# Four distances, modulo 256 bytes, between the pieces of an expert's first weights and the tokens that stream past them

## The chip, the cores and the metric

The kernel runs on one core of a Trainium2 chip. The metric is device time in microseconds of one execution. A core has TensorE (matmuls: PE in the profile, its weight loads PEld), VectorE (DVE), ScalarE (ACT), GpSimd (POOL) and SyncE (SP, which issues most DMAs), all working on SBUF, a memory of 128 partitions.

## The reference

Retention (linear attention with a decay) over 8 batches of 576 tokens and 8 heads of 64, and behind it a mixture of experts in which each of the 4608 tokens goes to one of 8 experts:

```python
scores = scale * np.matmul(q, k.transpose(0, 1, 3, 2))
ret = scores * Dmat[None]          # gamma ** (i - j), causal
x = np.matmul(ret, v)              # to (4608, 512)
e_idx = np.argmax(x @ w_gate, axis=1)
for e in range(8):                 # mask: the tokens of expert e
    h = np.maximum(x[mask] @ w1[e], 0.0)      # 512 -> 1024
    out[mask] = gate_w[mask, None] * eom[mask, e, None] * (h @ w2[e])
```

## The kernel before

A first stage does the retention in 36 chunks of 128 tokens, chooses the experts and scatters the tokens to a buffer sorted by expert. The second stage goes over the experts. An expert has 616 slots for tokens, in two parts: part 0 of 360 columns and part 1 of 256. Its first product, `mm1`, goes over 8 blocks `fb` of 128 hidden features; its second, `mm2`, over 5 tiles `t` of tokens (four of 128 and, at t = 2, one of 104) and the 8 blocks `fb`.

To get near full precision every operand is held as a high part and the rest (`h` and `l` in the names), and each product is three matmuls on fp32r data: high by high, high by low, low by high. So a call of `mm1` is 12 matmuls (4 blocks `k` of 128 input features by 3), of 360 columns or of 256; a block `fb` of an expert is 12 of each, one part after the other; and an expert has 192 of them, all experts 1536. In a matmul the stationary operand (`lhsT`) is first loaded into the array by a weight load of 128 columns; then the moving operand (`rhs`) streams past. The weight load for the next matmul runs while the current one streams. In `mm1` the weights `w1` are stationary and the tokens `x` (tiles `xh`, `xl`) move; in `mm2` the hidden values (`hh`, `hl`) are stationary and `w2` moves, 512 columns.

`w1` of an expert comes in four pieces `fp` of 256 hidden features: the blocks fb = 2 fp and 2 fp + 1 read piece fp. `start_w` (L128) issues the DMA of a piece into a staging tile `st` and takes two tiles of 4096 bytes per partition from the pool `wpool`, `w1h{fp}` and `w1l{fp}`; `hi_w` (ACT, L142) and `lo_w` (DVE, L147) fill them. The pool has one buffer for each name, so all 8 experts use the same addresses. It lays out tiles in the order in which they are first asked for: the four pieces of `w1`, then the four of `w2` (`wsched` in the first stage gives that order).

Where in 256 bytes a tile begins is set by three small tiles that nothing reads: `shift0` (64 bytes, in the pool ahead), `shift1` (192 bytes, between the pieces of `w1` and of `w2`) and `shift2` (128 bytes, before `x` of part 0). With them the addresses per partition are, modulo 256: all eight `w1` tiles 128 (`w1h0` at 54400), all `w2` tiles 64 (`w2h0` at 87360), `x` of both parts 64 (141120 and 196672), the hidden tiles of both parts 64. Steps inside these tiles are multiples of 512 bytes. So in every matmul of `mm1` the stationary operand begins 64 bytes beyond the moving one, in every one of `mm2` 0 bytes, counted modulo 256.

In the first stage `xnat` (L529) multiplies the retention's output `xT` (stationary, at 224 modulo 256) by `iw` (moving, at 160 for its first block p = 0, and 576 bytes further with each of four blocks p, so at 160, 224, 32 and 96); these matmuls are fp32, not fp32r, and are two passes each.

Of the kernel before, what the change touches and what calls it, by code (L numbers as in the profile page):

```python
# [10 lines left out]
F32 = mybir.dt.float32  # L11
# [15 lines left out]
P = 128  # L27
# [21 lines left out]
def tile_retention_moe(  # L49
# [21 lines left out]
    wpool = ctx.enter_context(tc.tile_pool(name="wpool", bufs=1))  # L71
# [50 lines left out]

    const.tile([P, 16], F32, name="shift0")
    W1, W2 = {}, {}

    def start_w(which, e, fp):  # L128
        src, shape = (w1, [P, KB, 256]) if which == 1 else (w2, [P, 2, DM])
        st = wst.tile(shape, F32, name="st")  # L130
        SP.dma_start(out=st, in_=src[e, fp].rearrange("p (a b) -> p a b", a=shape[1]))
        if which == 2 and not W2:
            wpool.tile([P, 48], F32, name="shift1")
        hi = wpool.tile(shape, F32R, name=f"w{which}h{fp}")
        lo = wpool.tile(shape, F32R, name=f"w{which}l{fp}")
        (W1 if which == 1 else W2)[e, fp] = (hi, lo)
        return st, hi, lo
# [11 lines left out]
    def load_w(which, e, fp):  # L149
        w = start_w(which, e, fp)  # L150
        hi_w(*w)
        lo_w(*w)
# [399 lines left out]
    def weights(g):  # L552
        for w, at in wsched.items():
            if g == at[0]:
                wparts[w] = start_w(w[0], 0, w[1])
            if g == at[1]:
                hi_w(*wparts[w])
# [161 lines left out]
    for t in range(TA, CT):  # L719
        load_rows(0, t)  # L720
    load_idx(0, 1)
    w = [start_w(1, 1, fp) for fp in range(2)]
    fill_slots(1)
    fill_slots(0)
# [56 lines left out]
    with ExitStack() as octx:  # L781
# [3 lines left out]
        with tc.For_i(0, n, 1) as i:  # L785
            e = nc.values_load(ovt[0:1, 0, bass.ds(i, 1)], engines=[mybir.EngineType.SP], min_val=0, max_val=E - 1)
# [102 lines left out]
```

## Time and profile before

| | us |
|---|---|
| median of 3 runs | 608.34 (608.02 to 609.44) |
| profiled execution | 608.83 |
| span of its profile | 607.0 |
| PE busy | 592.4 |
| weight loads (PEld) busy | 529.0 |
| DVE / ACT / POOL busy | 332.8 / 219.3 / 188.1 |

The span goes from the first to the last instruction of the program; the profiled execution has 1.8 us outside it. [...] What a matmul costs the engine is read from start to start. [...]

### The profile page before, as it was taken

The page shows a single profiled execution, that of the slowest core. Times are in us where ns is not written, and L with a number is a line of the kernel's source. Part 1 is how long each engine was busy: PE and PEld are TensorE (multiplying, and loading weights), DVE is VectorE, ACT ScalarE, POOL GpSimd, SP SyncE. Part 2 cuts the span into 40 slices and gives each one's busy share as a digit, 9 for nine tenths or more (in the row PEclk, how much of TensorE's full clock was granted, in tenths as well). Part 3 has the DMA queues.
Part 4 walks back from the last instruction along what each step waited for, and adds up shares of the span by engine and source line. Part 5 has one row for each costly group of instructions (what it writes and reads, how often), then busy time and mean ns, then how long its engine had stood idle before and what let it go on. Part 6 is the DMA issues. An engine that isn't in the chain of part 4 may idle for free. (4 is left out here: it accounts for less than half of the span.)

```text
span 607.0 us, 13986 instructions
## 1 busy us (share of the span) xinstructions
PE 592.4 (98%) x5688; PEld 529.0 (87%) x5688; DVE 332.8 (55%) x735; ACT 219.3 (36%) x477; POOL 188.1 (31%) x235
## 2 busy tenths in 40 slices
PE   8999999999999999999999999999999999999995
PEld 5889888878898999879978987997899799889974
DVE  4599888898760666624543554445265435625410
ACT  1334433323331545324433443433354344325110
POOL 2245544575457515016013301601250110110011
PEclk9999999999999999999999999999999999999999
DMA  9989989875225676444343534444262334221011
GB/s 307 357 301 318 331 289 342 322 265 201 97 91 185 182 197 198 130 128 136 109 138 116 175 104 136 118 136 139 94 188 94 115 107 143 103 84 52 1 38 42
DMA packets 56925, 100.28 MB, mean 165 GB/s; under 512 B 14967, under 2 KB 35832, under 8 KB 56860
## 3 DMA queue, kind: packets, MB, share of 16 engines
q1 hardware_dynamic: 46988, 76.72, 39.6%
q0 software_dynamic: 9440, 21.60, 9.8%
q8 instruction: 45, 0.74, 0.5%
q10 hardware_dynamic: 432, 1.05, 0.5%
q14 instruction: 20, 0.16, 0.1%
HBM read 77.75 MB, written 31.18 MB: 179 GB/s over the span
## 5 line engine op out<-in xcount | busy, mean ns | idle before, releaser
L262 PE MATMUL h_ps<-xh,w1h 128*128 128x360 f32 (+1 forms) x512 | 155.2, 303 | 0.1
L262 PE MATMUL h_ps<-xh,w1l 128*128 128x360 f32 (+1 forms) x512 | 154.9, 303 | 0.0
L262 PE MATMUL h_ps<-xl,w1h 128*128 128x360 f32 (+1 forms) x512 | 154.8, 302 | 0.0
L289 POOL DMA_INDIRECT out_dram<-y,idx x40 | 39.8, 994 | 313.4 <-ACT y L288 268.0
L270 DVE SCALAR_TENSOR_TENSOR hl<-h_ps,hh 128x360 fp32r<-128x360 f32 (+1 forms) x128 | 61.2, 478 | 128.8 <-ACT hh L269 114.4
L283 PE MATMUL y_ps<-w2h,hh 128*128 128x512 f32 (+1 forms) x320 | 125.0, 390 | 0.0
L283 PE MATMUL y_ps<-w2l,hh 128*128 128x512 f32 (+1 forms) x320 | 124.9, 390 | 0.0
L283 PE MATMUL y_ps<-w2h,hl 128*128 128x512 f32 (+1 forms) x320 | 124.6, 389 | 0.0
L269 ACT ACTIVATE hh<-h_ps 128x360 fp32r<-128x360 f32 (+1 forms) x128 | 55.0, 430 | 117.7 <-PE h_ps L262 113.1
L262 PEld LDWEIGHTS h_ps<-xh,w1h 128*128 128x128 f32 x512 | 96.0, 188 | 0.6 <-DVE xl L245 0.3
L262 PEld LDWEIGHTS h_ps<-xl,w1h 128*128 128x128 f32 x512 | 96.1, 188 | 0.3
L262 PEld LDWEIGHTS h_ps<-xh,w1l 128*128 128x128 f32 x512 | 96.1, 188 | 0.0
L288 ACT ACTIVATE y<-y_ps,idx 128x512 f32<-128x512 f32 (+1 forms) x40 | 27.6, 690 | 138.6 <-issue 90.0
L147 DVE TENSOR_TENSOR w1l<-st,w1h 128x512 fp32r<-128x512 f32 x64 | 44.9, 739 | 48.4 <-ACT w1h L142 47.0
L283 PEld LDWEIGHTS y_ps<-w2h,hl 128*128 128x128 f32 (+1 forms) x320 | 58.8, 184 | 14.1
L283 PEld LDWEIGHTS y_ps<-w2h,hh 128*128 128x128 f32 (+1 forms) x320 | 58.8, 184 | 13.8
L283 PEld LDWEIGHTS y_ps<-w2l,hh 128*128 128x128 f32 (+1 forms) x320 | 58.7, 184 | 13.6
L194 POOL DMA_INDIRECT xs<-xgrp,sli x36 | 38.8, 1077 | 62.2 <-issue 21.3
L194 POOL DMA_INDIRECT xs<-zx,fill x42 | 46.1, 1099 | 7.1 <-issue 6.5
L352 POOL TENSOR_TENSOR vp<-pk,gk_sb 128x512 f32<-128x512 f32 x36 | 37.7, 1049 | 30.8 <-PE st_ps L392 12.2
L376 DVE TENSOR_TENSOR S_sb<-sc,cmat_sb 128x512 f32<-128x512 f32 x64 | 41.1, 684 | 11.2 <-PE sc L365 10.7
L147 DVE TENSOR_TENSOR w2l<-st,w2h 128x512 fp32r<-128x512 f32 x64 | 44.7, 737 | 2.3
(128 smaller groups left out, 675.1 us busy)
## 6 DMA issues: line engine op xcount, KB each, us to landing
st<-in_w_dram SPq DMA_DIRECT2D x64, 512.0 KB
pk<-in_pack_dram SPq DMA_DIRECT2D x32, 768.0 KB
x_q<-xs SPq DMA_DIRECT2D x140, 64.0 KB
kn<-in_krow_dram SPq DMA_DIRECT2D x14, 256.0 KB
gq_sb<-in_gq_dram SPq DMA_DIRECT2D x5, 256.0 KB
pk<-in_pack_dram SPq DMA_DIRECT2D x4, 256.0 KB
pk<-in_pack_dram SPq DMA_DIRECT2D x2, 512.0 KB
x_g<-xs SPq DMA_DIRECT2D x4, 256.0 KB
```

The source lines that it names most:

```text
L147: V.tensor_tensor(out=lo[:, k], in0=st[:, k], in1=hi[:, k].bitcast(F32), op=ALU.subtract)
L194: i = G.indirect_dma_start(out=xs, out_offset=bass.IndirectOffsetOnAxis(ap=at, axis=0), in_=x, in_offset=None, **({} if bound is None else ...
L262: i = T.matmul(ps, lhsT=a[:, k, :], rhs=b[:, k, 0:n], start=(j == 0), stop=(j == 3 * KB - 1))
L269: A.activation(out=hh, in_=ps, func=AF.Relu)
L270: V.scalar_tensor_tensor(out=hl, in0=ps, scalar=0.0, in1=hh.bitcast(F32), op0=ALU.max, op1=ALU.subtract)
L283: i = T.matmul(ps, lhsT=a[:, n], rhs=b, start=(j == 0), stop=(j == 3 * FB - 1))
L288: A.activation(out=y, in_=ps, func=AF.Copy, scale=idx.bitcast(F32)[0:m, e, t, 1:2])
L289: G.indirect_dma_start(out=out, out_offset=bass.IndirectOffsetOnAxis(ap=idx[0:m, e, t, 0:1], axis=0), in_=y, in_offset=None, bounds_check= ...
L352: G.tensor_tensor(out=vs[g], in0=pk[g][:, 2].rearrange("p (h d) -> p h d", h=H), in1=gk_sb[:, g % CPB].broadcast_to([P, H, D]), op=ALU.mult)
L376: V.tensor_tensor(out=v(S_sb[:, r].rearrange("p a i -> p (a i)")), in0=v(sc[:, r]), in1=cmat_sb[:, 1:3].rearrange("p c a i -> p a (c i)"). ...
```

## The change

`shift1` goes. In its place three tiles of 64 bytes that nothing reads are taken from the same pool, one before each of the pieces 1, 2 and 3 of `w1`. The pieces then begin at 128, 192, 0 and 64 modulo 256, which is 64, 128, 192 and 0 beyond `x`. The three tiles have 192 bytes together, as `shift1` had, so `w2` and all that follows keep their addresses. No instruction is added, removed or moved.

```diff
     def start_w(which, e, fp):
         src, shape = (w1, [P, KB, 256]) if which == 1 else (w2, [P, 2, DM])
         st = wst.tile(shape, F32, name="st")
         SP.dma_start(out=st, in_=src[e, fp].rearrange("p (a b) -> p a b", a=shape[1]))
-        if which == 2 and not W2:
-            wpool.tile([P, 48], F32, name="shift1")
+        if e == 0 and which == 1 and fp > 0:
+            wpool.tile([P, 16], F32, name=f"shift_{fp}")
         hi = wpool.tile(shape, F32R, name=f"w{which}h{fp}")
         lo = wpool.tile(shape, F32R, name=f"w{which}l{fp}")
```

## Rows read from the trace of the kernel before

**Rows 1.** The page: busy time by engine, share, instructions; the clock by slices.

```profile
PE 592.4 (98%) x5688; PEld 529.0 (87%) x5688; DVE 332.8 (55%) x735; ACT 219.3 (36%) x477; POOL 188.1 (31%) x235
...
PEclk9999999999999999999999999999999999999999
```

**Rows 2.** Busy time by stretch: length, PE, PEld, DVE, ACT, POOL, clock, DMA.

```profile
215.00:600.00 385.00, 384.94 (x2207) 346.67 (x2205) 179.61 (x300) 144.33 (x285) 79.71 (x86) 1.00 0.38 117
```

**Rows 3.** Groups by line and shape: count, busy us, mean ns, idle before.

```profile
L262 PEld LDWEIGHTS h_ps<-xl,w1h 128*128 128x128 f32 x512 | 96.1, 188 | 0.3
...
L262 PE MATMUL h_ps<-xh,w1h 128*128 128x360 f32 x256 | 84.0, 328 | 0.1
...
L262 PE MATMUL h_ps<-xh,w1h 128*128 128x256 f32 x256 | 71.1, 278 | 0.0
```

**Rows 4.** Order of time on PE (start, length), expert 0, 256-column matmuls alone.

```profile
199.35 0.28 PE L262 MATMUL h_ps<-xh,w1h 128*128 128x256 f32 x1
199.47 0.28 PE L262 MATMUL h_ps<-xl,w1h 128*128 128x256 f32 x1
...
207.51 0.28 PE L262 MATMUL h_ps<-xh,w1h 128*128 128x256 f32 x1
```

**Rows 5.** The same view: expert 3, fb = 0, part 1.

```profile
330.43 0.28 PE L262 MATMUL h_ps<-xl,w1h 128*128 128x256 f32 x1
330.55 0.28 PE L262 MATMUL h_ps<-xh,w1l 128*128 128x256 f32 x1
...
331.73 0.33 PE L262 MATMUL h_ps<-xh,w1h 128*128 128x360 f32 x1
```

**Rows 6.** The same view: expert 1, a block of part 0.

```profile
227.04 0.33 PE L262 MATMUL h_ps<-xh,w1h 128*128 128x360 f32 x1
227.21 0.33 PE L262 MATMUL h_ps<-xl,w1h 128*128 128x360 f32 x1
...
228.54 0.28 PE L262 MATMUL h_ps<-xh,w1h 128*128 128x256 f32 x1
```

**Rows 7.** The same view: `mm2`, the tile of 104 tokens and the one behind.

```profile
257.63 0.39 PE L283 MATMUL y_ps<-w2h,hh 128*104 128x512 f32 x1
...
263.13 0.40 PE L283 MATMUL y_ps<-w2h,hh 128*128 128x512 f32 x1
263.36 0.40 PE L283 MATMUL y_ps<-w2l,hh 128*128 128x512 f32 x1
263.60 0.39 PE L283 MATMUL y_ps<-w2h,hl 128*128 128x512 f32 x1
...
265.21 0.39 PE L283 MATMUL y_ps<-w2h,hh 128*128 128x512 f32 x1
...
273.82 0.39 PE L283 MATMUL y_ps<-w2h,hl 128*128 128x512 f32 x1
```

**Rows 8.** All of line 529: shortest, middle and longest row in ns.

```profile
L529 PEld LDWEIGHTS xa<-iw,xT x144: 186/190/192, 15.5 to 167.2; 128*128 128x128 f32 x144
L529 PE MATMUL xa<-iw,xT x144: 284/286/390, 15.6 to 167.3; 128*128 128x144 f32 x144
L529 PEld LDWEIGHTS xb<-iw,xT x144: 190/190/190, 16.0 to 167.7; 128*128 128x128 f32 x144
L529 PE MATMUL xb<-iw,xT x144: 286/286/286, 16.1 to 167.8; 128*128 128x144 f32 x144
```

**Rows 9.** Groups by line and shape, as in Rows 3: the writers of the weights.

```profile
L147 DVE TENSOR_TENSOR w1l<-st,w1h 128x512 fp32r<-128x512 f32 x64 | 44.9, 739 | 48.4 <-ACT w1h L142 47.0
L147 DVE TENSOR_TENSOR w2l<-st,w2h 128x512 fp32r<-128x512 f32 x64 | 44.7, 737 | 2.3
...
L142 ACT CAST w1h<-st 128x512 fp32r<-128x512 f32 x64 | 36.4, 620 | 0.0
L142 ACT CAST w2h<-st 128x512 fp32r<-128x512 f32 x64 | 36.3, 619 | 0.0
```

## The prediction

> **What bounds the kernel now.** Read the page's busy times first: PE has work in flight for 98% of the span, and the clock is at its full level (2.4 GHz) in every slice [rows 1]. The table by stretch sharpens this for the stage of the experts: from 215 to 600 us PE is busy in 384.94 of 385.00 us, while DVE, ACT and POOL are busy in 179.61, 144.33 and 79.71 [rows 2]. So in this stage nothing but TensorE sets the time, and every nanosecond that the change puts on a matmul of `mm1`, or takes off it, is a nanosecond of the span. Since no instruction changes, the only question is the pace of these matmuls.
>
> A row's length doesn't give the pace (278 ns for a 256-column matmul and 328 ns for a 360-column one, [rows 3], overlap their neighbours). The order of time does, from start to start:
> - 256 columns, many alike in a row: from 199.35 to 207.51 us there are 72, so 113.3 ns each [rows 4].
> - 360 columns: from 227.04 to 228.54 us there are 9, so 166.7 ns [rows 6].
> - 512 columns in `mm2`, once settled: 38 in 8.61 us, so 226.6 ns [rows 7].
>
> The 256 and the 512 are in proportion to their columns (twice 113.3 is 226.6), though `mm1` has its operands 64 bytes apart and `mm2` 0. In proportion, 360 columns would take 113.3 x 360/256 = 159.3 ns. They take 7.4 ns more.
>
> **Where the place of an operand could show.** While one matmul streams `x`, the weights of the next are read from the same partitions, in every matmul. Two places in the trace show that the two reads together cost something that neither has alone.
> - The same 256-column matmuls, with the same addresses, also run slower: in the first block of expert 3 there are 11 from 330.43 to 331.73 us, 118 ns each [rows 5] against 113.3 [rows 4]. The clock is full and nothing is waited for. The slow pace lasts through this block and is gone in the next; the first block of each of the experts 1 to 7 has it, which makes seven. So the pair of reads has at least two ways to run side by side, 4.7 ns apart.
> - In `mm2`, weight loads of 104 columns, less to read, go with a slower stream: from 257.63 to 263.13 us 24 matmuls, 229.2 ns each against 226.6. Behind them the 128-column loads start at 235 ns (two from 263.13 to 263.60) and settle to 226.6 only from 265.21 on [rows 7].
>
> Here the Trainium skill speaks against any effect of the change: "SBUF — State Buffer", in "Who interferes with whom", gives TensorE two independent read ports, one for the moving operand and one for weight loads, and says that TensorE never waits on anyone. By that rule the sum of the change would be 0 and the time the one of before. The trace doesn't agree in full: the paces of 118 and 229.2 ns [rows 5, 7] are waits of TensorE's reads that it leaves unexplained.
>
> **The change part by part.**
> - *`shift1` goes, three tiles of 64 bytes come.* Nothing reads or writes them: no instruction, 0 us. Since 3 x 64 = 192 bytes are what `shift1` had, `w2` and the hidden tiles stay 0 apart and the 960 matmuls of `mm2` keep their pace: 0 us.
> - *The writers of the weights.* ACT and DVE write the moved tiles. Today they write `w1` at 128 and `w2` at 64 modulo 256, in 620 against 619 ns and 739 against 737 ns [rows 9]: the place doesn't show, 0 us. If it did, DVE's and ACT's idle time in the stage [rows 2] would hide it. The DMA lands in `st`, which isn't moved.
> - *Piece 0* keeps its 64 bytes: 192 matmuls of each length, 0 us.
> - *Pieces 1, 2 and 3* go to 128, 192 and 0: 3 x 192 = 576 matmuls of 256 columns and 576 of 360. No fp32r matmul of `mm1` in this trace has such a distance, so its price is bounded by rows.
>  - 256 columns: the lower bound is 0, since 113.3 is already in proportion to the 512-column matmuls; the upper is what the worst rows of `mm2` have over their settled pace, 235 - 226.6 = 8.4 ns. Nearest is the slow pace of these very matmuls, 4.7 ns: their stream and the weight load of 128 columns beside it are about equally long, so a disturbed load has little room. I take 4.7: 576 x 4.7 ns = 2.7 us.
>  - 360 columns: between -7.4 (the excess over proportion goes) and +8.4 ns. I take 0. The weight load is the same 128 columns and has 166.7 - 113.3 = 53 ns more room here, so a delay of the load is hidden; a delay of the stream is not, which is why the upper bound stays.
>
> Sum: +2.7 us. On the profiled execution that is 608.83 + 2.7 = 611.5; its own time is 0.5 above the median of the runs, so against the median 608.34 + 2.7 = 611.0 us.
>
> **The rivals.**
> - *The place doesn't matter (608.3).* For it: `xnat`, where the stationary operand lies 64, 0, 192 and 128 beyond the moving one for p = 0 to 3, all four distances of the change. Both pairs have the same middle row, 286 ns, and the same weight load, 190 ns; in the pair at 192 and 128 shortest and longest agree too [rows 8]. The equal pace for each column in `mm1` at 64 and `mm2` at 0 says the same. Against it: these are fp32 matmuls of 144 columns, so the stream is short beside its weight load, and a collision in the longer fp32r streams could pass unseen there; and the two paces of 256 columns [rows 4, 5] differ in nothing but how the reads fall. It decides if the reads settle clear of each other from any start, as the 512-column ones do behind 265.21 us.
> - *The other side: 64 is the poor distance for 360 columns (604.0).* The mechanism: in each 360-column matmul the stream runs once into the weight load beside it and waits 7.4 ns, and at the other distances it doesn't. Price: 576 x 7.4 ns = 4.3 us less, 608.3 - 4.3 = 604.0; with two of the three pieces clear, 384 x 7.4 = 2.8 us less, 605.5. It decides where the gain on the 360 columns exceeds what the 256 lose, that is from 2.7 us, 4.7 ns a matmul. Against it: 256 columns at the same 64 have no such excess, and 360 is the one length that isn't a multiple of 64 columns (256 bytes), so the excess may be its own, whatever the distance.
> - *The forecast, but larger.* Both lengths pay: 4.7 ns on the 256 and 8.4 on the 360 gives 576 x 13.1 ns = 7.5 us, 615.9. This is the upper part of the case slower.
> - *The unread tiles get no room.* Then all pieces would stay at 64 and `w2` alone would move by 192. `shift0` and `shift2` are unread too and stand in the addresses of before; under 0.01, left out.
>
> **How the numbers follow.** Slower (the reads collide at some of the new distances) 0.50; the place doesn't matter 0.32; 64 was the poor one 0.18. I lean to slower over same because there is a second pace [rows 5] with nothing but the meeting of the two reads to explain it, and to slower over faster because the 256 columns have nothing to gain. About 0.2%, 1.2 us, is what a measurement of this kernel can tell from no change; the cases' times lie beyond that on either side, so their chances are those of faster, same and slower. The likeliest time is 611.0. The range goes from 605.5 (two of three pieces gain) to 616.0 (both lengths pay), which leaves out some 0.15 at the two ends.
>
> **What the profile afterwards would show.** Each piece can be read by itself: for fb >= 1 a pair of blocks (12 of 360 columns and 12 of 256) takes 12 x (166.7 + 113.3) = 3360 ns now. Blocks 0 and 1 should keep it; blocks 2 and 3, 4 and 5, 6 and 7 show the price of 128, 192 and 0. By the forecast their 256-column starts are about 118 ns apart and the 360-column ones 166.7; by the first rival all stay at 113.3 and 166.7; by the second the 360 go towards 159.3. The pace of `mm2` should stay at 226.6, the clock full, and PE busy without a gap. The prediction is wrong if blocks 0 and 1 or `mm2` change, if PE gets idle time, or if the price sits in the 360 columns while the 256 keep their pace.

## The result and the profile after

The changed kernel takes 610.14 us (median of 22 runs, 609.50 to 613.17) against 608.85 for the kernel before, measured beside it (22 runs, 607.28 to 610.61). The ratio is 1.0026, 95% interval 1.0019 to 1.0033: 1.6 us slower, between 1.2 and 2.0 (the two medians differ by 1.3). The forecast was 2.7 us slower.

The profiled execution took 609.85 us with a span of 608.1. The page's row of busy times, the row of the stage of the experts, and the groups that answer to [rows 3, 9] (all lines are one further down in the changed kernel):

```profile
PE 593.6 (98%) x5688; PEld 530.5 (87%) x5688; DVE 331.3 (54%) x735; ACT 218.9 (36%) x477; POOL 188.8 (31%) x235
```

```profile
215.00:600.00 385.00, 385.00 (x2201) 347.38 (x2200) 178.89 (x299) 143.40 (x284) 79.54 (x86) 1.00 0.38 117
```

```profile
L263 PE MATMUL h_ps<-xh,w1h 128*128 128x360 f32 x256 | 84.0, 328 | 0.1
...
L263 PE MATMUL h_ps<-xh,w1h 128*128 128x256 f32 x256 | 71.9, 281 | 0.0
...
L148 DVE TENSOR_TENSOR w1l<-st,w1h 128x512 fp32r<-128x512 f32 x64 | 44.9, 738 | 48.4 <-ACT w1h L143 47.0
...
L143 ACT CAST w1h<-st 128x512 fp32r<-128x512 f32 x64 | 36.4, 619 | 0.0
```

As in [rows 1, 2] the stage is TensorE's from end to end, with the clock at its full level, 2.4 GHz (the 1.00 behind POOL's time). Counts are the same; the writers of the weights have their old durations (738 and 619 ns). Only the mean row of a 256-column matmul has moved, from 278 to 281 ns.

What each piece pays is read as the prediction proposed, from the start of one block to the start of the next. In expert 4, blocks fb = 1, 2, 4 and 6 (order of time on PE: start in us, length, operation):

```profile
386.06 0.33 PE L263 MATMUL h_ps<-xh,w1h 128*128 128x360 f32 x1
...
388.05 0.28 PE L263 MATMUL h_ps<-xh,w1h 128*128 128x256 f32 x1
...
389.42 0.32 PE L263 MATMUL h_ps<-xh,w1h 128*128 128x360 f32 x1
...
391.38 0.28 PE L263 MATMUL h_ps<-xh,w1h 128*128 128x256 f32 x1
...
392.81 0.32 PE L263 MATMUL h_ps<-xh,w1h 128*128 128x360 f32 x1
...
396.20 0.33 PE L263 MATMUL h_ps<-xh,w1h 128*128 128x360 f32 x1
...
398.18 0.28 PE L263 MATMUL h_ps<-xh,w1h 128*128 128x256 f32 x1
...
399.60 0.33 PE L263 MATMUL h_ps<-xh,w1h 128*128 128x360 f32 x1
...
403.00 0.33 PE L263 MATMUL h_ps<-xh,w1h 128*128 128x360 f32 x1
...
404.98 0.28 PE L263 MATMUL h_ps<-xh,w1h 128*128 128x256 f32 x1
...
406.42 0.33 PE L263 MATMUL h_ps<-xh,w1h 128*128 128x360 f32 x1
```

Each block is 12 matmuls. From 404.98 to 406.42 twelve of 256 columns at distance 0 take 1.44 us, where twelve at 64 take 1.37 (388.05 to 389.42). All blocks of expert 4, taken to the nanosecond from the same starts (ns for 12 of 360 columns, 12 of 256, and the pair):

| blocks fb | distance | before | after |
|---|---|---|---|
| 0 | 64 | 1999 + 1415 = 3414 | 1998 + 1415 = 3413 |
| 1 | 64 | 1989 + 1372 = 3361 | 1990 + 1375 = 3365 |
| 2 and 3 | 128 | 1988 + 1372 = 3360, both | 1964 + 1421 = 3385; 1968 + 1425 = 3393 |
| 4 and 5 | 192 | 1988 + 1372 = 3360, both | 1984 + 1416 = 3400; 1991 + 1414 = 3405 |
| 6 and 7 | 0 | 1988 + 1372 = 3360, both | 1977 + 1435 = 3412; 1979 + 1435 = 3414 |

The other experts from 1 to 7 repeat this to a few ns. So the six moved blocks pay 8546 - 8232 = 314 ns on their 256 columns and get back 11928 - 11863 = 65 ns on their 360, 249 ns net; in seven experts 1.74 us.

Expert 0 shows the two lengths apart from each other, since its blocks of one part follow one another. First 360 columns at distance 0 (fb = 7), then 256 columns at 64, 128, 192 and 0 (fb = 1, 3, 5 and 7):

```profile
177.65 0.32 PE L263 MATMUL h_ps<-xh,w1h 128*128 128x360 f32 x1
...
179.57 0.39 PE L284 MATMUL y_ps<-w2h,hh 128*128 128x512 f32 x1
...
198.29 0.28 PE L263 MATMUL h_ps<-xh,w1h 128*128 128x256 f32 x1
...
199.65 0.28 PE L263 MATMUL h_ps<-xh,w1h 128*128 128x256 f32 x1
...
201.07 0.28 PE L263 MATMUL h_ps<-xh,w1h 128*128 128x256 f32 x1
...
202.49 0.28 PE L263 MATMUL h_ps<-xh,w1h 128*128 128x256 f32 x1
...
203.91 0.28 PE L263 MATMUL h_ps<-xh,w1h 128*128 128x256 f32 x1
...
205.32 0.28 PE L263 MATMUL h_ps<-xh,w1h 128*128 128x256 f32 x1
...
206.76 0.29 PE L263 MATMUL h_ps<-xh,w1h 128*128 128x256 f32 x1
...
208.20 0.40 PE L284 MATMUL y_ps<-w2h,hh 128*128 128x512 f32 x1
```

Twelve of 256 take 1.36, 1.42, 1.41 and 1.44 us (113.7, 118.2, 117.8 and 120.1 ns each, from the starts to the nanosecond); twelve of 360 at distance 0 take 1.92, which is 160.0 ns each against 166.7 at 64 [rows 6]. Over expert 0 the 256 columns cost 392 ns more than before and the undisturbed 360-column blocks (fb = 3, 4, 6, 7) 202 ns less. Together 1.74 + 0.39 - 0.20 = 1.9 us, within the interval of what was measured. About 0.1 us of the 0.20 is the luck of this execution: in three other traces the blocks at distance 0 (fb = 6 and 7), at the same addresses and behind the same instructions, took 1973 to 1978 ns and not 1920 (see the two parts at different distances). The two profiled spans differ by 1.1 us only, because in this execution expert 1 began 0.7 us earlier (219.10 against 219.78 us).

### The profile page after: what moved, and what is told of

The parts are those of the page before. It is cut to its first block, busy times and chain, and to the rows that moved or that the text cites. A ratio compares the mean times of both kernels' runs of the same rounds, so it can differ in the third digit from the quotient of the medians.

```text
span 608.1 us, 13986 instructions
## 1 busy us (share of the span) xinstructions
PE 593.6 (98%) x5688; PEld 530.5 (87%) x5688; DVE 331.3 (54%) x735; ACT 218.9 (36%) x477; POOL 188.8 (31%) x235
```

## The experiments

Two questions were open: whether it is the distance of the two operands that sets the pace, and not the piece or the place of one operand; and whether the reason given for the price, that only the weight load is delayed and a 256-column matmul has no room to hide it, is the right one. In the table of distances below, (a, b) means that the weights lie a bytes beyond `x` of part 0 (360 columns) and b beyond `x` of part 1 (256 columns), modulo 256.

### The distances dealt to other pieces

`shift0` goes and a fourth tile of 64 bytes stands before `w2`: pieces 0 to 3 at 0, 64, 128, 192.

```diff
-    const.tile([P, 16], F32, name="shift0")
...
-        if which == 2 and not W2:
-            wpool.tile([P, 48], F32, name="shift1")
+        pad = {(1, 1): 16, (1, 2): 16, (1, 3): 16, (2, 0): 16}.get((which, fp)) if e == 0 else None
+        if pad:
+            wpool.tile([P, pad], F32, name=f"shift_{which}{fp}")
```

> The same four distances as in the changed kernel, dealt to other pieces: pieces 0 to 3 at 0, 64, 128 and 192. Theory of the distance: the pairs of blocks of the pieces take about 3413, 3360, 3390 and 3402 ns, the dear pair moves from piece 3 to piece 0; time as the changed kernel, 1 to 2 us over before. Rival (the price sits in the piece, by its place in the row of blocks or in SBUF): the order stays as in the changed kernel, 3360, 3388, 3402 and 3413 for pieces 0 to 3.

Measured: 608.50 us in one run, 606.22 before; pairs of blocks in expert 4: 3353 and 3404 (distance 0), 3376 and 3365 (64), 3385 and 3392 (128), 3400 and 3405 (192). The blocks at 128 and 192 have the same times as in the changed kernel, to 1 ns, though they are other pieces. So it is not the piece. But the dear pair didn't simply move to piece 0: where 3413 was forecast its blocks took 3353 and 3404, and the dearest piece is now the one at 192. The rows (blocks fb = 0 and 1 of expert 4, both at 0) show where the first one gained:

```profile
381.61 0.32 PE L262 MATMUL h_ps<-xh,w1h 128*128 128x360 f32 x1
...
383.53 0.28 PE L262 MATMUL h_ps<-xh,w1h 128*128 128x256 f32 x1
...
384.96 0.33 PE L262 MATMUL h_ps<-xh,w1h 128*128 128x360 f32 x1
...
386.94 0.28 PE L262 MATMUL h_ps<-xh,w1h 128*128 128x256 f32 x1
```

The same 360-column matmuls with the same distance take 1.92 us for twelve behind `mm2` and 1.98 behind 256-column ones. At one distance there is more than one steady pace, and here they go with what ran before.

### Everything 64 bytes further

`shift0` has 128 bytes in place of 64, the three tiles of the change stand between the pieces, and a tile of 192 bytes behind `x` of part 1 moves that pool and the hidden values of part 1 as well. Distances as in the changed kernel, every operand of the experts 64 bytes further.

```diff
-    const.tile([P, 16], F32, name="shift0")
+    const.tile([P, 32], F32, name="shift0")
...
+        pad = {(1, 1): 16, (1, 2): 16, (1, 3): 16}.get((which, fp)) if e == 0 else None
...
+            if e == 0 and part == 1:
+                pl.tile([P, 48], F32, name="shift4")
```

> The distances of the changed kernel piece by piece (64, 128, 192, 0), but w1, x, w2 and the hidden values all lie 64 bytes further in 256. Theory of the distance: every pair of blocks as in the changed kernel within 5 ns (3365, 3385 to 3392, 3400 to 3405, 3413), mm2 at 226.6 ns a matmul. Rival (the place in 256 bytes of one operand by itself decides): the pace of a piece follows the address of w1, so piece 1 (now at 0) shows the 3402 of the piece that was at 0, piece 2 (now at 64) the 3413, and piece 3 (now at 128) the 3360.

Measured: 607.25 us in one run, 606.22 before. Pairs in expert 5: 3413, 3365, 3385, 3392, 3400, 3405, 3413, 3413, the changed kernel's numbers within 1 ns, as in the other experts from 1 to 7. Block fb = 6 of expert 4, whose piece is now at 128 modulo 256, the address that all pieces had before:

```profile
400.38 0.33 PE L265 MATMUL h_ps<-xh,w1h 128*128 128x360 f32 x1
...
402.36 0.28 PE L265 MATMUL h_ps<-xh,w1h 128*128 128x256 f32 x1
...
403.79 0.33 PE L265 MATMUL h_ps<-xh,w1h 128*128 128x360 f32 x1
```

It takes 1.98 and 1.43 us all the same. In these experts the address of one operand by itself doesn't matter; the distance does. Expert 0 differs: there 256 columns at 64 took 1413 and 1416 ns (1372 and 1364 in the changed kernel) and 360 at 0 1973 and 1974 (1920). These are second paces that other kernels show too (below), so they don't speak for the address, but this run alone can't rule it out there. Since the stationary operand is read by weight loads alone, the likely cause is the meeting of a weight load with a stream; no row shows the meeting itself.

### Part 0 at 0, part 1 at 64

The best pace that each length has shown alone, combined: `shift0` and `shift1` go, which puts the weights at 64 like `x` of part 0, and `x` of part 1 goes 64 bytes down.

```diff
-    const.tile([P, 16], F32, name="shift0")
...
-        if which == 2 and not W2:
-            wpool.tile([P, 48], F32, name="shift1")
...
+            if e == 0 and part == 1:
+                pl.tile([P, 16], F32, name="shift4")
...
+        if (e, part, fb) == (0, 1, FB - 1):
+            pools["ht1"].tile([P, 48], F32, name="shift5")
```

> All four pieces of w1 lie 0 bytes (modulo 256) beyond x of part 0 and 64 beyond x of part 1; mm2 keeps its 0. Theory of the distance (the pace of a matmul follows from the distance of its own two operands): the 360-column matmuls go at the 160.0 ns that the blocks 6 and 7 of expert 0 show in the changed kernel, the 256-column ones stay at 113.3; a pair of blocks falls from 3360 to 3280 ns, 56 pairs and expert 0 together give about 5 us less than before, 603.7 us. Rival (the neighbours decide: in experts 1 to 7 of the changed kernel the 360-column matmuls at 0 went at 164.9 ns): a pair of 1978 + 1360 = 3338 ns and 1.2 to 1.8 us less, 607 us. Rival (only the piece, not the distance): no change, 608.8 us.

Measured: 604.29 us (10 runs) against 606.22 (13 runs of the kernel before beside it), ratio 0.9963, 95% interval 0.9947 to 0.9979: 2.2 us faster, the best kernel of this study, but less than half of the 5 us that the distance by itself would give. The rows of expert 0 (360 columns, then 256) and of block fb = 3 of expert 4:

```profile
169.15 0.33 PE L263 MATMUL h_ps<-xh,w1h 128*128 128x360 f32 x1
...
171.12 0.33 PE L263 MATMUL h_ps<-xh,w1h 128*128 128x360 f32 x1
...
201.21 0.28 PE L263 MATMUL h_ps<-xh,w1h 128*128 128x256 f32 x1
...
202.57 0.28 PE L263 MATMUL h_ps<-xh,w1h 128*128 128x256 f32 x1
...
390.83 0.32 PE L263 MATMUL h_ps<-xh,w1h 128*128 128x360 f32 x1
...
392.75 0.28 PE L263 MATMUL h_ps<-xh,w1h 128*128 128x256 f32 x1
...
394.16 0.32 PE L263 MATMUL h_ps<-xh,w1h 128*128 128x360 f32 x1
```

In expert 4 the 360 columns run at 1.92 us for twelve and the 256, at the 64 that gave 1.36 in expert 0, at 1.41, the slow pace of [rows 5]. In expert 0 it is the other way round: the 360 at the slower of their two paces (1.97), the 256 at 1.36. The pair in experts 1 to 7 is 3333 ns, neither the 3280 of the first theory nor the 3338 of the second, which had the slower pace on the other length. Both paces of both lengths exist at these distances; alternating, the two lengths don't reach their better one together.

### The two parts at different distances

The changed kernel's four pieces, with `x` of part 1 moved by 128, 64 and 192 bytes (a tile behind it as above, of 32, 16 and 48 elements, and one behind the hidden values that keeps them in place).

> w1 in the four pieces of the changed kernel, x of part 1 moved by 128 bytes, so that the distances of the 360- and the 256-column matmuls are (64,192), (128,0), (192,64) and (0,128) for pieces 0 to 3; mm2 keeps 0. Theory of the distance by itself: a pair of blocks is the sum of the two blocks as they run alone in expert 0 of the kernels so far (360 columns: 2000 at 64, 1967 at 128, 1993 to 2002 at 192, 1920 at 0; 256 columns: 1360, 1418, 1415, 1441): 3415, 3408, 3355 and 3338 ns. Theory of the distance and the entry (each distance has more than one steady way to run, and what ran before decides which): 256 at 64 at 1413 instead of 1360 and 360 at 0 at 1974 instead of 1920 may come up, 3408 and 3392 for pieces 2 and 3. Time within 2 us of before.

> As the kernel with the parts 128 apart, but by 64: distances (64,128), (128,192), (192,0) and (0,64). Sum of blocks alone: 3418, 3382, 3441 and 3280 ns; with the entry deciding, piece 3 repeats the 1920 + 1413 = 3333 that all four pieces showed where part 0 lay at 0 and part 1 at 64. Time 1 to 2 us over before.

> As before it, by 192: distances (64,0), (128,64), (192,128) and (0,192). Sum of blocks alone: 3441, 3327, 3418 and 3335 ns; with the entry deciding, piece 1 may take 3380 and piece 3 up to 3389. Time within 2 us of before.

Measured: 610.61, 610.25 and 610.64 us, one run each, 609.23 before. Pairs in expert 4, both blocks of a piece (the forecast's sum of blocks alone ahead):

| apart | piece 0 | piece 1 | piece 2 | piece 3 |
|---|---|---|---|---|
| 128 | (64,192) 3415: 3415, 3403 | (128,0) 3408: 3399, 3398 | (192,64) 3355: 3370, 3364 | (0,128) 3338: 3355, 3396 |
| 64 | (64,128) 3418: 3423, 3411 | (128,192) 3382: 3408, 3384 | (192,0) 3441: 3419, 3424 | (0,64) 3280: 3357, 3399 |
| 192 | (64,0) 3441: 3422, 3411 | (128,64) 3327: 3343, 3364 | (192,128) 3418: 3407, 3411 | (0,192) 3335: 3388, 3392 |

The sum of blocks alone holds to 30 ns except where 0 for the 360 columns or 64 for the 256, the two that have shown two paces, is part of the pair. There it fails by up to 119 ns, and (0,64) takes 3357 and 3399 here but 3333 in the kernel above, where all pieces have it. So the distance alone doesn't decide. The second theory, distance and entry, has the right kind of answer but few of its numbers: 3396 came for 3392 and 3388 and 3392 for 3389, but 3370 and 3364 for 3408, 3343 and 3364 for 3380, and (0,64) didn't repeat its 3333. The times are 1.0 to 1.4 us over before, a single run against a single run.

Expert 0 shows more. Up to the end of its part 0 these three kernels, the changed one and the one with shorter loads below run the same instructions on the same addresses. The blocks at 0 (fb = 6 and 7) begin just behind a wait of TensorE for VectorE, 0.19 to 0.20 us in all five. They took 1920 and 1920 ns in the changed kernel and in the one 64 apart, but 1978 and 1973 or 1974 in the other three, here 128 apart (fb = 6, then fb = 7):

```profile
176.72 0.33 PE L267 MATMUL h_ps<-xh,w1h 128*128 128x360 f32 x1
...
178.70 0.33 PE L267 MATMUL h_ps<-xh,w1h 128*128 128x360 f32 x1
```

So behind a wait neither the addresses nor the order of instructions fixes the pace. What is left is when the matmuls start, which no run here sets.

### A longer part 0

Part 0 with 384 columns, distances as in the changed kernel.

```diff
-CAP = 616
-CA = 360
+CAP = 640
+CA = 384
```

> The distances of the changed kernel, and 384 columns in part 0 in place of 360 (640 slots for an expert instead of 616, so 24 columns more in each matmul of part 0 and a third tile of 128 tokens in mm2; the result is the same). If the 7.4 ns over proportion that 360 columns have at 64 are their own, because 360 isn't a multiple of 64 columns, then 384 columns run at 113.3 x 384/256 = 170.0 ns at 64 and at every other distance. If they belong to the distance, 384 columns run over 170 at 64 (about 177) and near 170 at 0. Time: 24 columns at 0.4427 ns x 768 matmuls = 8.2 us more than the changed kernel, and mm2's tile at 226.6 instead of 229.2 ns.

Measured: 616.63 us in one run, 609.23 before, 7.4 us more; 8.2 over the changed kernel was expected. Twelve alone in expert 0, at 128 (fb = 3) and at 0 (fb = 7):

```profile
169.61 0.34 PE L263 MATMUL h_ps<-xh,w1h 128*128 128x384 f32 x1
...
171.72 0.34 PE L263 MATMUL h_ps<-xh,w1h 128*128 128x384 f32 x1
...
178.58 0.33 PE L263 MATMUL h_ps<-xh,w1h 128*128 128x384 f32 x1
...
180.66 0.39 PE L284 MATMUL y_ps<-w2h,hh 128*128 128x512 f32 x1
```

That is 175.5 and 173.3 ns each; at 64 and 192 it is 173.4 and 173.3 once settled. No distance reaches the proportional 170.0, and none stands out as 64 did for 360 columns. Neither half of the expectation holds: 384 columns have 3.3 ns or more over proportion at every distance, so the excess depends on the length as well as on the distance.

### The second weights at four distances, and at 64

In the first kernel the tiles of 64 bytes stand between the pieces of `w2`, so that the hidden values lie 192, 128, 64 and 0 beyond them; in the second all pieces of `w2` lie 64 bytes lower (a tile of 128 bytes before them in place of 192, and 64 more before `x` of part 0). `w1` and `x` keep their 64.

```diff
-        if which == 2 and not W2:
-            wpool.tile([P, 48], F32, name="shift1")
+        pad = {(2, 1): 16, (2, 2): 16, (2, 3): 16}.get((which, fp)) if e == 0 else None
...
```

```diff
-        if which == 2 and not W2:
-            wpool.tile([P, 48], F32, name="shift1")
+        pad = {(2, 0): 32}.get((which, fp)) if e == 0 else None
...
-    xta.tile([P, 32], F32, name="shift2")
+    xta.tile([P, 48], F32, name="shift2")
```

> w1 as before; the four pieces of w2, which move in mm2, go to places where the hidden values lie 192, 128, 64 and 0 beyond them. A matmul of mm2 streams 512 columns beside a weight load of 128. Theory as predicted (only the load is delayed, and beside a long stream that is hidden): 226.6 ns at every distance, 5.44 us for a tile of 24 matmuls, no change in time. Rival (the stream itself waits at some distances, as the 360-column matmuls between 160 and 167 ns suggest): the six matmuls of a piece differ by 1 to 8 ns from piece to piece, up to 3/4 of 960 x 4 ns = 2.9 us more.

> w1 and x as before; all pieces of w2 64 bytes lower, so that the stationary hidden values lie 64 bytes beyond the moving w2 in every matmul of mm2, in place of 0. Theory as predicted (a load of 128 columns beside 512 is hidden): settled pace 226.7 ns, 5440 ns for a tile of 24, no change in time. Rival (the stream waits): another settled pace, by the steps of 6.67 ns seen so far between 226.7 and 233.3 ns, so up to 5600 ns a tile, and up to 960 x 6.7 ns = 6.4 us more in all.

Measured: 610.71 us (606.22 before) and 612.02 us (608.66 before), one run each. The tile t = 3 of expert 4 in the changed kernel, where `mm2` is as before, and in the second of these:

```profile
426.24 0.40 PE L284 MATMUL y_ps<-w2h,hh 128*128 128x512 f32 x1
...
431.72 0.39 PE L284 MATMUL y_ps<-w2h,hh 128*128 128x512 f32 x1
```

```profile
427.27 0.39 PE L284 MATMUL y_ps<-w2h,hh 128*128 128x512 f32 x1
...
432.87 0.39 PE L284 MATMUL y_ps<-w2h,hh 128*128 128x512 f32 x1
```

24 matmuls take 5.48 us at 0 (with the unsettled first ones of [rows 7]; 5.44 settled) and 5.60 at 64, 233.3 ns each. With the four distances mixed, this tile takes 5.55: its pieces, at 192, 128, 64 and 0, take 1374, 1397, 1400 and 1380 ns for six. So 512 columns pay as well, 6.7 ns a matmul, though the load of 128 columns beside them has over 100 ns of room (226.7 - 113.3). The reason that the prediction gave, a delay of the load that a longer stream hides, falls. That the stream itself waits is what is left; it is argued, since no row shows the wait.

The second kernel also shows what the entry does. `w1` and `x` are at the addresses of before and only `mm2` has changed. Yet the 256 columns of expert 0, 113.3 ns each in [rows 4], now take 1413 to 1419 ns a block, about 117.8 each. In experts 1 to 7 it is the other way round: the first block of part 1 takes 1372 where it took 1415. The block fb = 1 of expert 0:

```profile
198.12 0.28 PE L263 MATMUL h_ps<-xh,w1h 128*128 128x256 f32 x1
...
199.53 0.28 PE L263 MATMUL h_ps<-xh,w1h 128*128 128x256 f32 x1
```

### Shorter loads

The changed kernel with a stationary operand of 64 columns in eleven of twelve 256-column matmuls; it leaves out their products for the other 64 hidden features.

```diff
-                i = T.matmul(ps, lhsT=a[:, k, :], rhs=b[:, k, 0:n], start=(j == 0), stop=(j == 3 * KB - 1))
+                c = P if part == 0 or j == 0 else 64
+                i = T.matmul(ps[0:c], lhsT=a[:, k, 0:c], rhs=b[:, k, 0:n], start=(j == 0), stop=(j == 3 * KB - 1),
+                             skip_group_check=True)
```

> The changed kernel, but in part 1 eleven of the twelve matmuls of a block use only 64 columns of w1 as the stationary operand (the first uses all 128), so their products for the other 64 hidden features are left out. The weight load beside a 256-column stream is then half as long and has about 53 ns of room. Theory as predicted (the load is delayed, and the 256-column matmul pays because it has no room): with this room all distances run alike, 113 ns or less, 1360 ns or less for a block alone in expert 0. Rival (the stream itself has to wait when it meets the load): the blocks still differ with the distance, by 20 ns or more for 12 matmuls, though a shorter load is met less often.

Measured: 609.56 us in one run, 608.66 before. Twelve alone in expert 0, at 64 (fb = 1) and at 0 (fb = 7):

```profile
198.63 0.28 PE L264 MATMUL h_ps<-xh,w1h 128*128 128x256 f32 x1
...
200.05 0.28 PE L264 MATMUL h_ps<-xh,w1h 128*128 128x256 f32 x1
...
207.03 0.28 PE L264 MATMUL h_ps<-xh,w1h 128*128 128x256 f32 x1
...
208.40 0.40 PE L286 MATMUL y_ps<-w2h,hh 128*128 128x512 f32 x1
```

1.42 us at 64, 1.40 at 128 and 192, 1.37 at 0: the distances still differ by 51 ns, and their order has turned round (1.36 and 1.44 at 64 and 0 with full loads). The two paces of 256 columns at 64 don't explain it: in experts 1 to 7 the short loads take 1429 to 1435 ns at 64, where full loads took 1360 to 1419 in any trace, and 1366 to 1380 at 0 in all experts, against 1422 to 1446. Room doesn't make the price vanish; another length of the load makes another distance the good one.

### Half steps

Pieces at distances 32, 96, 160 and 224: `shift0` goes, tiles of 32, 64, 64, 64 bytes stand before the pieces of `w1` and one of 32 before `w2`.

> The four pieces of w1 at distances 32, 96, 160 and 224 from x of both parts, halfway between the distances tried so far. So far every steady pace is a whole number of 6.67 ns (16 columns, 64 bytes) over one or a few matmuls: 113.3, 166.7, 226.7, 160.0, 120.0, 3 x 117.8. If the reads meet by lines of 64 bytes, a weight block that begins in the middle of a line touches 9 lines for 128 columns in place of 8, and no distance of the four should give the 113.3 alone that 64 gives: 256 columns at 117 to 120, 360 at 160 to 167, pairs between 3380 and 3420, time 1 to 3 us over before. If only the distance by itself counts, smoothly, each half step lies between its neighbours: 256 columns alone near 1400, 1389, 1416 and 1428 for 12 (from 1441, 1360, 1418, 1415), 360 alone near 1960, 1983, 1983 and 1957.

Measured: 610.57 us in one run, 607.84 before. Pairs in expert 4: 3412 and 3420 (32), 3401 and 3395 (96), 3434 twice (160), 3373 twice (224). Twelve of 256 columns alone, in the order of the pieces: about 1418, 1407, 1437, 1400 ns. At 160 (fb = 4):

```profile
204.27 0.28 PE L262 MATMUL h_ps<-xh,w1h 128*128 128x256 f32 x1
...
205.71 0.28 PE L262 MATMUL h_ps<-xh,w1h 128*128 128x256 f32 x1
```

None is the 1360 that 64 gives, as the theory of lines said. But that is weak support: 64 itself gave 1360 to 1364 in five traces with full loads and 1413 to 1418 in six. 160 lies outside what its neighbours 128 and 192 span (1418, 1415), against the smooth one. The bounds set for the pairs, 3380 to 3420, were too narrow on both sides. That 64-byte lines are the reason isn't shown by this, only that 32 bytes matter.

## Why the prediction was right, point by point

- *TensorE alone sets the time, and only `mm1` of the moved pieces changes.* Right: blocks 0 and 1 changed by 1 and 4 ns, the settled `mm2` not at all, and what the blocks add up to (1.9 us) is what was measured (1.2 to 2.0).
- *256 columns: 4.7 ns, the slow pace of [rows 5].* Right in size: 4.1 ns at 128 and 4.4 at 128's second block, 3.7 and 3.5 at 192, 5.3 at 0, from the blocks in alternation (1421, 1425, 1416, 1414, 1435 against 1372). Over all experts 7 x 0.314 + 0.392 = 2.6 us, where 2.7 was forecast. That the size came so close is partly luck: 4.7 was a second pace at 64, and no row said that the other distances would cost as much.
- *360 columns: 0.* Here the sum was mis-sized. They get 7 x 0.065 + 0.20 = 0.7 us back, within the bounds of the prediction (-7.4 to +8.4 ns a matmul), but not 0. This is the difference between 2.7 and about 2; as told above, about 0.1 of the 0.7 hung on this execution.
- *The reason for taking 0, a delayed load that a longer stream hides, was wrong.* 512 columns pay 6.7 ns at 64, and 256 columns with half as long a load still pay by distance. Every length tried depends on the distance, whatever its room, which points to the stream as what waits. That the 256 columns lose and the 360 gain comes from where 64 happened to stand for each: the best of four for the one (in its faster pace, which the kernel before has in nearly all blocks), the poorest or next to it for the other.
- *The first rival, that the place doesn't matter,* fell. The rule of the Trainium skill ("SBUF — State Buffer", "Who interferes with whom") that TensorE's two read ports are independent and that it never waits would give no change; the blocks disagree with it by up to 54 ns in 3360, and the measurement decides. Its row evidence, the even rows of `xnat` at four distances [rows 8], was about fp32 matmuls of 144 columns and didn't carry over to these fp32r ones; whether for the type or the length isn't shown.
- *The second rival, that 64 is poor for 360 columns,* had the right direction and size for 360 columns by themselves, in their better pace (160.0 against 166.7 at distance 0 in expert 0, 6.7 ns of the 7.4), and lost because in alternation they gained little (0.8 to 2.0 ns at 128 and 0, at most 0.3 at 192) and the 256 columns cost more. That the stream meets the load just once, as it supposed, isn't shown. Moving part 0 alone brought it out: 2.2 us faster than before.
- What decides between two steady paces at one distance isn't settled. What ran before bears on it (behind `mm2`, behind the other length), and behind a wait the same instructions on the same addresses have taken either pace. By which step is open.

## What to carry to other kernels

Where weight loads run beside streams without a gap, the distance of the stationary from the moving operand modulo 256 bytes is worth some per cent of a matmul, and an unread tile of 64 bytes sets it at no other cost. Read it from start to start in the trace, for each length by itself and then in the order in which the kernel runs them, since the best distance of one length isn't that of another and paces depend on what ran before. One kernel with a different distance for each piece measures four of them at once; but take more than one trace, since the same distance can run at either of two paces.

## What the runs showed of the hardware that was not expected

- The even paces seen of these fp32r matmuls, those with all starts equally far apart, are whole numbers of 6.67 ns, which at 2.4 GHz are 16 cycles: 113.3 and 120.0 ns are 17 and 18 of them, 160.0 and 166.7 are 24 and 25, 173.3 is 26, 226.7 and 233.3 are 34 and 35. The others don't go by such steps from matmul to matmul: at 117.8 ns the starts lie 117 to 119 apart, and 256 columns at 0 in expert 0 of the changed kernel repeat 118, 121, 120, 124 and 117, 120.0 in the mean.
- One set of addresses has several steady paces: 256 columns at 64 run at 113.3 or 117.8 ns, 360 columns at 0 at 160.0 or 164.4 (1920 or 1973 ns for twelve), each for as long as nothing else comes between. At 0 behind a wait either has come up with the same instructions and addresses.
- Half as long a weight load made 256 columns at 64 slower: 1418 to 1435 ns for twelve, against 1360 to 1419 with full loads, and at 0 faster: 1366 to 1380 against 1422 to 1446.
